# Attention and a gated feed-forward block on one core: more gate products by the seven-product form, their quarters in other buffers, and GpSimd for some of the elementwise work

## The chip, the cores and the metric

The kernel runs on one core of one Trainium2 chip. The metric is device time in microseconds (us). Five engines work side by side, each through its own queue in order: TensorE (PE in profiles, with its weight loads as PEld), VectorE (DVE), ScalarE (ACT), GpSimd (POOL) and SyncE (SP, which here issues DMAs). An instruction waits in its engine's queue until the instructions on other engines that it depends on have ended, and everything behind it in that queue waits too.

## The reference

Inputs are q, k and v of shape (8 batches, 8 heads, 576 positions, 64) and three weights. Attention is causal in a window: heads 0 to 3 see the last 32 positions, heads 4 to 7 every fourth of the last 128. Its output, as 4608 tokens of 512, goes through a gated block:

```python
scores = scale * np.matmul(q, k.transpose(0, 1, 3, 2))
...
attn = attn / (np.sum(attn, axis=-1, keepdims=True) + 1e-09)
return np.matmul(attn, v)
...
g = x @ w_gate                                  # (4608, 512) @ (512, 1536)
gelu = 0.5 * g * (1.0 + erf(g * inv_sqrt2))
val = x @ w_val
return (gelu * val @ w_out)                     # (4608, 1536) @ (1536, 512)
```

## The kernel before

The 4608 tokens are cut into nine chunks of 512 (`CH`). Attention of a batch is computed on TensorE in 64 x 64 tiles, spread over the output phase of the chunk before it is needed; the last batch's falls in chunk 6. x is kept transposed in `x_all` (shown as xT): features on partitions, tokens in columns.

A chunk has two phases. In the gate phase the 12 blocks nb of 128 hidden units are computed. A block done directly takes four matmuls of 512 columns for the gate value (word "g": then a gelu on ScalarE from the PSUM bank) and four for the other factor (word "u": then VectorE multiplies gelu and factor from the bank into `u_all`). The two banks of a block come from `gate_banks`. In the output phase `u_all` is multiplied by w_out.

From chunk 1 on, the output product is done pair by pair (two blocks are a pair j) in a form with seven block products in place of eight. It needs sums of u, made by VectorE in `u_sums` (words "k"; `ux`), and the seven products run in the order 1, 7, 6, 4, 5, 2, 3, twelve matmuls of 256 columns each.

The same form is used for some gate pairs, those in `IN_SEVEN`. Per pair `ffn1_seven` emits seven groups (words "f", in the order 1, 2, 6, 7, 5, 4, 3) of four 256-column matmuls, 28 in place of 16 of 512 columns. The groups need sums of the weights (`gate_sums`, words "h", made once in a chunk before, in columns of x_all that are no longer used) and of x (`x_sums`, word "x", once for each chunk, again in freed columns). A group's result lies in one PSUM bank and `quarter_out` takes it out: products 1, 6 and 7 are copied by ScalarE into a saved buffer (`snap`, shown as vdiag and turned); products 2, 5 and 4 are added by VectorE to one of these into a quarter (128 x 512: 256 columns of gate, 256 of the other factor); product 3 is copied by ScalarE into a quarter. One group later `quarter_gelu` puts the gelu of a quarter's first half on ScalarE, and one group after that `quarter_u` multiplies it by the other half into u_all. Within a pair the groups alternate between two banks, and a group that starts a bank anew must wait until the last result there has been read.

The order of everything is written out by hand: `gate_words` and `out_words` give a string of words for each chunk, a number standing for so many matmuls, and `run_program` emits them one by one into the engines' queues.

Of the kernel before, what the change touches and what calls it, by code (L numbers as in the profile page):

```python
# [10 lines left out]
F32 = mybir.dt.float32  # L11
# [6 lines left out]
USCALE = 8.0  # L18
# [3 lines left out]
def kernel(  # L22
# [605 lines left out]
    IN_SEVEN = {c: (1,) if c < 7 else (1, 2) for c in range(3, NCH)}  # L628
    sums_at = {1: 0, 2: 2 * CH}
# [10 lines left out]

    def gate_sums(j, part):

        for m in range(2):
# [8 lines left out]
            nc.vector.tensor_tensor(out_, first, other, op)  # L652
# [9 lines left out]
    def x_sums(c):  # L662
# [3 lines left out]
        for out_, first, other in ((t2, b12, b11), (t1, b22, t2), (t3, b22, b12), (t4, b21, t1)):  # L666
            nc.vector.tensor_tensor(out_, first, other, ALU.subtract)
# [26 lines left out]
    def quarter_out(c, j, kind, bank):  # L694

        src, kept = ps[:, bank, :], {1: 0, 6: 1, 7: 2}.get(kind)
        if kept is not None:
            nc.scalar.copy(snap[kept], src)
            return
        t = osbp.tile([P, DM], F32, tag="osb", name="quarter")  # L700
        if kind == 3:
            nc.scalar.copy(t, src)
        else:
            nc.vector.tensor_tensor(t, src, snap[{2: 0, 4: 1, 5: 2}[kind]], ALU.add)  # L704
        nb, half = 2 * j + (kind in (4, 5)), int(kind in (3, 5))
        tiles.setdefault("ready", []).append((nb, half, t))

    def quarter_gelu():

        for nb, half, t in tiles.pop("ready", []):  # L710
            g = ffn.tile([P, 2 * P], F16, tag="gq")
            nc.scalar.activation(g, t[:, 0 : 2 * P], AF.Gelu)  # L712
            tiles.setdefault("gated", []).append((nb, half, t, g))

    def quarter_u():

        for nb, half, t, g in tiles.pop("gated", []):
            dst = u_all[:, nb, 2 * P * half : 2 * P * half + 2 * P]
            by = -USCALE if nb % 2 else USCALE
            nc.vector.scalar_tensor_tensor(dst, g, by, t[:, 2 * P : 4 * P], ALU.mult, ALU.mult)  # L720
# [223 lines left out]
    def gate_banks(c, nb):  # L944
# [3 lines left out]
        if c in IN_SEVEN:  # L948
            return (1, 4) if nb in ((1, 9, 11) if c < 7 else (1, 11)) else (0, 7)
# [33 lines left out]
    def run_program(c, words, mms, banks):  # L983
# [3 lines left out]
        for word in words.split():  # L987
# [27 lines left out]
            elif kind == "f":  # L1015
                j, product, place = args
                ffn1_seven(c, j, product, (1, 4)[place], product in (1, 2, 7))
                quarter_u()
                quarter_gelu()
                quarter_out(c, j, product, (1, 4)[place])  # L1020
# [31 lines left out]
    def gate_words(c):  # L1052
# [121 lines left out]
```

## Time and profile before

| | |
|---|---|
| runs | 321.05 us median of 3 (321.03 to 321.54) |
| profiled execution | 320.39 us, span 318.7 us, TensorE clock 1.00 |
| TensorE busy | 309.1 us, 97% of the span |
| VectorE busy | 240.5 us, 75% |
| ScalarE busy | 181.2 us, 57% |
| GpSimd busy | 84.2 us, 26%; none of it after chunk 5 |

A row of the timeline gives start, duration, engine, line, operation and tiles, "x4" when rows were merged, and in brackets the idle time ahead of it with what ended it. In groups of instructions the numbers behind the first bar are busy time and the mean of one in ns.

### The profile page before, as it was taken

What the parts mean: (1) busy time and instruction counts of PE and PEld (TensorE: products, weight loads), DVE (VectorE), ACT (ScalarE), POOL (GpSimd) and SP (SyncE); (2) the same over time, 40 slices, a digit from 0 to 9 for tenths busy, and PEclk for the clock granted to TensorE, in tenths of its full rate; (3) what the DMA queues carried; (4) which work ended last, traced back from release to release, by engine and by line L of the source; (5) the groups of instructions that cost most, each with busy time, mean ns of one, the idle gap of its engine ahead of it and who ended that gap; (6) DMA issues with size and microseconds to landing.
All of it is one profiled execution on the core that took longest, in us unless ns stands there. A gap on an engine that the chain in (4) does not pass through costs nothing.

```text
span 318.7 us, 8755 instructions
## 1 busy us (share of the span) xinstructions
PE 309.1 (97%) x3585; PEld 192.6 (60%) x3585; DVE 240.5 (75%) x472; ACT 181.2 (57%) x295; POOL 84.2 (26%) x134
## 2 busy tenths in 40 slices
PE   7999999999999999999999999999999999999995
PEld 4754544446844576548654775578556856576664
DVE  6763656799757787698879886978789788946862
ACT  2673476536753477448754775567655777425740
POOL 8875603402364151160215111511000000000000
PEclk9999999999999999999999999999999999999999
DMA  8999997898699997996879638965100210030004
GB/s 188 183 203 206 205 202 149 264 187 204 159 283 154 225 210 168 241 246 159 215 165 263 157 114 194 239 146 147 35 3 1 80 56 0 2 109 25 0 0 134
DMA packets 110792, 47.17 MB, mean 148 GB/s; under 512 B 83616, under 2 KB 110240, under 8 KB 110752
## 3 DMA queue, kind: packets, MB, share of 16 engines
q1 hardware_dynamic: 97248, 38.29, 52.7%
q0 software_dynamic: 12944, 7.67, 17.0%
q10 hardware_dynamic: 560, 0.66, 0.8%
q8 instruction: 28, 0.46, 0.6%
q14 instruction: 12, 0.10, 0.1%
HBM read 37.75 MB, written 9.44 MB: 148 GB/s over the span
## 4 chain that ended last, share of the span: by engine, by line
PE 83%; DVE 9%; DMA 3%; ACT 2%; issue 2%; POOL 1%; DVEq 0%
PE ps L623 45%; PE ps L799 20%; PE ps L685 7%; PE ps L458 6%; PE ps L724 3%; DVE u_all L1007 2%; DMA xT<-in_k_dram 2%; DMA out_dram<-part 1%; DVE ux L760 1%; DVE ux L765 1%; PE ps L378 1%; DVE quarter L704 1%; DVE P L493 1%; ACT P L488 1%; DVE xT L652 1%
## 5 line engine op out<-in xcount | busy, mean ns | idle before, releaser
L1002 ACT ACTIVATE g<-ps 128x512 f16<-128x512 f32 x92 | 54.8, 597 | 73.8 <-PE ps L623 72.6
L623 PE MATMUL ps<-xT,wv 128*128 128x512 f16 x368 | 95.8, 379 | 0.7 <-DVE u_all L1007 0.7
L623 PE MATMUL ps<-xT,wg 128*128 128x512 f16 x368 | 95.0, 379 | 0.1
L1007 DVE SCALAR_TENSOR_TENSOR u_all<-g,ps 128x512 f16<-128x512 f16 x92 | 62.5, 684 | 33.4 <-PE ps L623 25.8
L623 PEld LDWEIGHTS <-wv 128*128 128x128 f16 x368 | 35.9, 98 | 38.6 <-issue 2.4
L623 PEld LDWEIGHTS <-wg 128*128 128x128 f16 x368 | 35.7, 98 | 38.5 <-issue 0.2
L799 PEld LDWEIGHTS <-u_all 128*128 128x128 f16 x390 | 36.8, 98 | 7.0 <-issue 1.0
L799 PE MATMUL ps<-wx,ux 128*128 128x256 f16 x288 | 35.8, 273 | 1.2 <-DVE ux L760 0.8
L799 PE MATMUL ps<-wo,u_all 128*128 128x256 f16 (+1 forms) x294 | 35.2, 271 | 0.0
L614 DVE TENSOR_TENSOR xT<-ps,rb 128x576 f16<-128x576 f32 x32 | 29.1, 939 | 4.4 <-PE ps L458 3.6
L488 ACT ACTIVATE P<-ps 128x832 f16<-128x832 f32 (+1 forms) x32 | 25.3, 835 | 11.8 <-PE ps L458 11.7
L799 PEld LDWEIGHTS <-ux 128*128 128x128 f16 x288 | 27.5, 98 | 5.8 <-DVE ux L760 1.4
L217 POOL CAST s<-stage 128x640 f16<-128x640 f32 x24 | 17.8, 767 | 47.3 <-DMA stage<-in_q_dram 34.3
L254 POOL CAST v<-stage 128x1152 f16<-128x1152 f32 x11 | 12.6, 1147 | 62.0 <-DMA stage<-in_v_dram 62.0
L760 DVE TENSOR_TENSOR ux<-u_all 128x512 f16<-128x512 f16 x48 | 22.1, 461 | 0.8
L585 ACT ACTIVATE lg<-ps 128x576 f32<-128x576 f32 x30 | 18.8, 656 | 6.7 <-PE ps L458 3.7
L685 PE MATMUL ps<-xT 128*128 128x256 f16 x128 | 18.8, 272 | 0.4 <-DVE quarter L704 0.4
L591 ACT ACTIVATE rb<-lg 128x576 f32<-128x576 f32 x30 | 19.0, 687 | 0.1
L712 ACT ACTIVATE g<-quarter 128x256 f16<-128x256 f32 x32 | 13.2, 414 | 9.3 <-DVE quarter L704 9.0
L229 POOL CAST s<-stage 128x512 f16<-128x512 f32 x24 | 15.9, 692 | 9.1 <-DMA stage<-in_q_dram 7.1
L685 PEld LDWEIGHTS <-xT 128*128 128x128 f16 x128 | 12.5, 97 | 7.7 <-issue 1.1
L765 DVE TENSOR_TENSOR ux<-u_all,ux 128x256 f16<-128x256 f16 (+1 forms) x44 | 15.9, 362 | 1.5
(104 smaller groups left out, 352.5 us busy)
## 6 DMA issues: line engine op xcount, KB each, us to landing
out_dram<-part SPq DMA_DIRECT2D x30, 256.0 KB, 3.4
stage<-in_v_dram SPq DMA_DIRECT2D x28, 144.0 KB, 3.6
stage<-in_q_dram SPq DMA_DIRECT2D x24, 128.0 KB, 3.5
stage<-in_k_dram SPq DMA_DIRECT2D x24, 128.0 KB, 3.0
stage<-in_q_dram SPq DMA_DIRECT2D x6, 512.0 KB, 4.8
stage<-in_k_dram SPq DMA_DIRECT2D x6, 512.0 KB, 5.2
stage<-in_v_dram SPq DMA_DIRECT2D x20, 128.0 KB, 2.9
wo<-in_moe_w_out_dram POOLq DMA_DIRECT2D x3, 512.0 KB, 16.6
```

Source lines behind the costliest of these rows:

```text
L458: nc.tensor.matmul(o[cols], lhs[rows], rhs[rows], start=st, stop=end, skip_group_check=True)
L488: nc.scalar.activation(pt[:, 0 : src.shape[1]], src, AF.Exp, bias=0.0, scale=scale)
L585: nc.scalar.activation(lg, psf[:, c0 : c0 + S], AF.Ln)
L591: nc.scalar.activation(rb, tiles.pop(("lg", n)), AF.Exp, scale=-1.0)
L614: nc.vector.tensor_tensor(dst, num, rb, ALU.mult)
L623: nc.tensor.matmul(ps[:, bank, :], w[:, kc, ns], xT[kc][:, tok], start=first, stop=end)
L685: nc.tensor.matmul(ps[:, bank, 2 * P * m : 2 * P * m + 2 * P], left[:, k], right[:, k], start=first and m == 0 and k == 0, stop=k == 1, sk ...
L760: nc.vector.tensor_tensor(ux[:, j, 0:2], k0, u_all[:, 2 * j : 2 * j + 2, hi], ALU.subtract)
L765: nc.vector.tensor_tensor(ux[:, at, 2], k0[:, :, lo], ux[:, at, 1], ALU.subtract)
L799: lambda o=o, s=s[:, P * p : P * p + P], t=t[:, c0:c1], st=st, end=end: nc.tensor.matmul(o, s, t, start=st, stop=end, skip_group_check=True)
L1002: nc.scalar.activation(g, ps[:, gate_banks(c, args[0])[0], :], AF.Gelu)
L1007: nc.vector.scalar_tensor_tensor(u_all[:, nb, :], tiles.pop(("g", nb)), -USCALE if c in SEVEN and nb % 2 else USCALE, val, ALU.mult, ALU.mult)
```

## The change

Gate pairs in the seven-product form: before, pair 1 in chunks 3 to 6, pairs 1 and 2 in chunks 7 and 8. Now pair 1 in chunks 3 to 5, pairs 1 and 2 in chunk 6, pairs 1, 2 and 3 in chunks 7 and 8. Pair 2's weight sums are made in chunk 5 (before: chunk 6), pair 3's in chunk 6. The scale of 8 or -8 that `quarter_u` applied is multiplied into the other factor's weights once for each pair (`scaled`, ScalarE), so that the product needs two inputs and no scalar. From chunk 6 the products of `quarter_u` and the x sums go to GpSimd, as do the weight sums of pairs 2 and 3. Quarters lie in the buffers tagged rb and lg, which attention uses in the output phase, and no longer in the four osb buffers, from which results are stored. Groups in banks 5 and 6 save their products in `stage`. The words are written as a table: a number of groups for each place, and what follows them.

```diff
-    IN_SEVEN = {c: (1,) if c < 7 else (1, 2) for c in range(3, NCH)}
-    sums_at = {1: 0, 2: 2 * CH}
+    ONE = ((1, (1, 4)),)
+    IN_PLACES = {c: ONE for c in range(3, 6)}
+    IN_PLACES[6] = ONE + ((2, (1, 4)),)
+    IN_PLACES[7] = IN_PLACES[8] = ONE + ((2, (5, 6)), (3, (5, 6)))
+    IN_SEVEN = {c: [j for j, _ in IN_PLACES[c]] for c in IN_PLACES}
+    sums_at = {1: 0, 2: 2 * CH, 3: 3 * CH}
+    free_pool = range(6, NCH)
...
+    def scaled(j):
+
+        for n in range(2):
+            i = next(i for i, (_, end) in enumerate(WC) if 2 * j * P < end)
+            at = (2 * j + n) * P - WC[i][0]
+            block = wv_t[i][:, :, at : at + P]
+            nc.scalar.activation(block, block, AF.Copy, bias=0.0, scale=-USCALE if n else USCALE)
+
     def gate_sums(j, part):
 
+        if part == 0:
+            scaled(j)
...
-            nc.vector.tensor_tensor(out_, first, other, op)
+            (nc.vector if j == 1 else nc.gpsimd).tensor_tensor(out_, first, other, op)
...
-            nc.vector.tensor_tensor(out_, first, other, ALU.subtract)
+            (nc.gpsimd if c in free_pool else nc.vector).tensor_tensor(out_, first, other, ALU.subtract)
...
         src, kept = ps[:, bank, :], {1: 0, 6: 1, 7: 2}.get(kind)
+        saved = snap if bank in (1, 4) else [stage[:, DM * i : DM * i + DM] for i in range(3)]
...
-        t = osbp.tile([P, DM], F32, tag="osb", name="quarter")
+        n = tiles["quarters"] = tiles.get("quarters", 0) + 1
+        t = nrm.tile([P, S], F32, tag=("rb", "lg", "rb", "lg", "rb")[n % 5], bufs=(3, 2, 3, 2, 3)[n % 5], name="quarter")[:, 0:DM]
...
-            by = -USCALE if nb % 2 else USCALE
-            nc.vector.scalar_tensor_tensor(dst, g, by, t[:, 2 * P : 4 * P], ALU.mult, ALU.mult)
+            (nc.gpsimd if c in free_pool else nc.vector).tensor_tensor(dst, g, t[:, 2 * P : 4 * P], ALU.mult)
...
-            return (1, 4) if nb in ((1, 9, 11) if c < 7 else (1, 11)) else (0, 7)
+            if nb in (1, 11) or (c < 6 and nb == 9):
+                return (1, 4)
+            return (5, 6) if c > 6 and nb % 2 and len(IN_SEVEN[c]) < 3 else (0, 7)
...
+    one = (
+        [0, 1, 1, 0, 1, 1, 0, 1, 1, 0, 1, 0, 0, 0, 0],
+        "||k0@0||k2@0||||k3@0|k3@1@2|k3@2@2|U|U k4@0|k1@0 k1@1@2|k1@2@2 k4@1 k4@2",
+    )
...
+    three = ([4, 4, 4, 3, 2, 2, 2], "k0@0||||k4@0|k1@0 k2@0|U k2@1@3")
+    three_mid, three_last = "U k2@2@3", "u11 k5@0 k3@0 k5@1@3 k5@2@3"
...
+    def seven_words(c):
+
+        pairs = IN_PLACES[c]
+        orders = [[f"f{j}@{product}@{banks[n % 2]}" for n, product in enumerate((1, 2, 6, 7, 5, 4, 3))] for j, banks in pairs]
+        pairs = [j for j, _ in pairs]
+        groups = orders[0] if len(pairs) == 1 else [w for both in zip(*orders[:2]) for w in both]
+        if pairs[1:] and orders[0][0][-1] == orders[1][0][-1]:
+            groups = orders[0] + orders[1]
+        groups += orders[2] if len(pairs) > 2 else []
...
```

A slot list such as that of `three` is read so: that many groups ahead of the first direct block's g, then that many after each of the following g and u words; the string between two bars is what follows the groups there.

ScalarE's queue in the gate phase of chunk 7, from the gelu of the block that follows block 1. "COPY vdiag", "COPY turned" and "COPY stage" are saved products 1, 6 and 7, "COPY quarter" is product 3, "g<-quarter" a quarter's gelu, "g<-ps" that of a direct block. Before:

```order
L1002 ACTIVATE g<-ps 128x512
L712 ACTIVATE g<-quarter 128x256 x2
L702 COPY quarter<-ps 128x512
L712 ACTIVATE g<-quarter 128x256
L698 COPY vdiag<-ps 128x512
L1002 ACTIVATE g<-ps 128x512
```

and now:

```order
L729 ACTIVATE g<-quarter 128x256 x3
L1020 ACTIVATE g<-ps 128x512
L729 ACTIVATE g<-quarter 128x256
L719 COPY quarter<-ps 128x512
L729 ACTIVATE g<-quarter 128x256
L719 COPY quarter<-ps 128x512
L729 ACTIVATE g<-quarter 128x256
L714 COPY stage<-ps 128x512
```

Two pairs' products come in turn, so that two copies of product 3 follow each other, each behind a gelu, and the second of them stands ahead of the copy of pair 3's product 1 (stage).

VectorE's queue at the end of the same phase. "u_all<-g,ps" is a direct block's u, "quarter<-ps" a quarter's sum, "ux<-u_all" and "u_all<-ux" are u sums. Before:

```order
L1007 SCALAR_TENSOR_TENSOR u_all<-g,ps 128x512
L760 TENSOR_TENSOR ux<-u_all 128x512
L765 TENSOR_TENSOR ux<-u_all,ux 128x256
L767 TENSOR_TENSOR u_all<-ux,u_all 128x256
L667 TENSOR_TENSOR xT<-xT 128x512 x4
```

and now:

```order
L721 TENSOR_TENSOR quarter<-ps,stage 128x512
L776 TENSOR_TENSOR ux<-u_all 128x512 x2
L1025 SCALAR_TENSOR_TENSOR u_all<-g,ps 128x512
L721 TENSOR_TENSOR quarter<-ps,stage 128x512
L781 TENSOR_TENSOR ux<-u_all,ux 128x3x256
L783 TENSOR_TENSOR u_all<-ux,u_all 128x3x256
L1025 SCALAR_TENSOR_TENSOR u_all<-g,ps 128x512
L776 TENSOR_TENSOR ux<-u_all 128x512 x2
L781 TENSOR_TENSOR ux<-u_all,ux 128x3x256
L783 TENSOR_TENSOR u_all<-ux,u_all 128x3x256
```

Quarter sums of pair 3 now stand among the last u words, the u sums of several pairs are one instruction, and the x sums are gone from here.

GpSimd's queue, whose last work before was the cast of v for the last batch, now goes on from there (chunk 6 and the first part of chunk 7):

```order
L254 CAST v_101<-stage 128x1152 x2
L682 TENSOR_TENSOR xT<-xT 128x512 x4
L736 TENSOR_TENSOR u_all<-g,quarter 128x256 x3
L667 TENSOR_TENSOR xT<-wg_90 128x256
L667 TENSOR_TENSOR xT<-wv_94 128x256
L667 TENSOR_TENSOR xT<-xT,wg_90 128x256
L667 TENSOR_TENSOR xT<-xT,wv_94 128x256
L736 TENSOR_TENSOR u_all<-g,quarter 128x256 x5
```

The x sums (L682) and the products of quarters (L736) came to it from VectorE, and the weight sums for pair 3 (L667) stand among the products of chunk 6.

62 lines of the change are left out of this document (30 added, 32 removed).

## The prediction

> **What bounds the kernel now.** I read the page first: busy shares, then the chain that ended last.
>
> ```profile
> PE 309.1 (97%) x3585; PEld 192.6 (60%) x3585; DVE 240.5 (75%) x472; ACT 181.2 (57%) x295; POOL 84.2 (26%) x134
> PE 83%; DVE 9%; DMA 3%; ACT 2%; issue 2%; POOL 1%; DVEq 0%
> ```
>
> TensorE (PE) is busy 97% of the span and holds 83% of the chain. So a column of matmul that goes is worth its time, and a wait that TensorE meets costs its whole length. Next came the chain in order of time, which prices TensorE's work (start, us, line, count; chunks 4 and 7):
>
> ```profile
> 156.40 4.32 PE ps L623 x20
> 259.31 0.87 PE ps L685 x8
> ```
>
> Twenty 512-column matmuls take 4.32 us, 0.216 each; eight of 256 columns 0.87, 0.1087 each, 0.435 for a group of four. These are the slots; the durations that single matmul rows show are longer because matmuls overlap. Then TensorE's rows in time: where a row starts later than the row before it plus its slots, TensorE waited.
>
> ```profile
> 129.56 1.03 PE L623 MATMUL ps<-xT,wv 128*128 128x512 f16 x4
> 131.00 0.60 PE L685 MATMUL ps<-xT 128*128 128x256 f16 x4 [0.41 <-DVE quarter L704]
> ...
> 136.20 1.03 PE L623 MATMUL ps<-xT,wg 128*128 128x512 f16 x4
> 137.92 1.02 PE L623 MATMUL ps<-xT,wv 128*128 128x512 f16 x4 [0.69 <-DVE u_all L1007]
> ...
> 169.66 1.03 PE L623 MATMUL ps<-xT,wg 128*128 128x512 f16 x4
> 170.72 1.02 PE L623 MATMUL ps<-xT,wv 128*128 128x512 f16 x4
> ...
> 245.65 1.03 PE L799 MATMUL ps<-wx,ux 128*128 128x256 f16 x8 [0.33 <-DVE vdiag L837]
> ...
> 254.75 1.11 PE L623 MATMUL ps<-xT,wv 128*128 128x512 f16 x4
> ...
> 276.33 1.25 PE L799 MATMUL ps<-wx,ux 128*128 128x256 f16 x10
> 278.01 1.70 PE L799 MATMUL ps<-wx,ux 128*128 128x256 f16 x14 [0.42 <-DVE ux L760]
> ...
> 284.79 1.03 PE L623 MATMUL ps<-xT,wg 128*128 128x512 f16 x4
> ...
> 305.22 1.47 PE L799 MATMUL ps<-wo,u_all 128*128 128x256 f16 x12
> ...
> 308.22 1.70 PE L799 MATMUL ps<-wx,ux 128*128 128x256 f16 x14 [0.43 <-DVE ux L760]
> ```
>
> By slots: chunk 3 loses 131.00 − (129.56 + 0.86) = 0.58 and 137.92 − (136.20 + 0.86) = 0.86, together 1.44; chunk 4 0.20 at 170.72 (chunk 5 I take at 0.15 by its likeness); chunk 6 0.5 at 245.65, where the wait is for VectorE's read of the bank. Chunk 7 runs from 254.75 to 284.79, 30.04; its work is 64 × 0.216 + 140 × 0.1087 = 29.0 (56 products of the gate, 84 of the output), so it waits 1.0, of which 278.01 − (276.33 + 10 × 0.1087) = 0.6 at the second output product. Chunk 8's gate phase takes 305.22 − 284.79 = 20.43 for 19.9 of work, and the same 0.6 follows: 1.1. In all 4.4 us stand in these chunks for the change to win, besides work.
>
> **The change, part by part.** *Work.* Three more pairs go by seven products (chunk 6 pair 2, chunks 7 and 8 pair 3): 28 × 0.1087 = 3.04 in place of 16 × 0.216 = 3.46, −0.42 each, −1.26 in all, on the path.
>
> *Banks.* Each group of products is read out of its PSUM bank by ScalarE or VectorE, and the next user of the bank waits for that. The written order now has such users directly behind each other. Chunks 3 to 5: the last product of pair 1 (product 3, bank 1) and then g9, which `gate_banks` puts into bank 1. Chunk 6: product 3 of pair 1, then product 1 of pair 2, both bank 1. Chunks 7 and 8: product 3 of pair 2, then product 1 of pair 3, both bank 5. Before, these alternate between banks. The price, from rows of chunk 7:
>
> ```profile
> 254.08 2.16 DVE L614 TENSOR_TENSOR xT<-ps,rb 128x576 f16<-128x576 f32 x2 [0.31 <-PE ps L458]
> 258.05 0.60 ACT L1002 ACTIVATE g<-ps 128x512 f16<-128x512 f32 x1 [0.59 <-PE ps L623]
> 258.28 1.03 PE L623 MATMUL ps<-xT,wg 128*128 128x512 f16 x4
> 259.34 0.60 ACT L1002 ACTIVATE g<-ps 128x512 f16<-128x512 f32 x1 [0.70 <-PE ps L623]
> 259.84 0.58 ACT L698 COPY vdiag<-ps 128x512 f32<-128x512 f32 x1
> 260.45 0.69 DVE L704 TENSOR_TENSOR quarter<-ps,vdiag 128x512 f32<-128x512 f32 x1 [1.08 <-ACT vdiag L698]
> 261.17 0.42 ACT L712 ACTIVATE g<-quarter 128x256 f16<-128x256 f32 x1 [0.76 <-DVE quarter L704]
> 261.52 0.58 ACT L698 COPY vdiag<-ps 128x512 f32<-128x512 f32 x1
> 262.00 0.59 ACT L698 COPY turned<-ps 128x512 f32<-128x512 f32 x1
> 263.31 0.69 DVE L704 TENSOR_TENSOR quarter<-ps,turned 128x512 f32<-128x512 f32 x1 [0.22 <-PE ps L685]
> 263.92 0.68 DVE L704 TENSOR_TENSOR quarter<-ps,vdiag 128x512 f32<-128x512 f32 x1
> ```
>
> TensorE's four matmuls from 258.28 end by slots at 259.14, the gelu on them starts 0.20 later. The copy takes 0.58; VectorE goes on 0.03 after it ends. Starts follow each other by 0.50 after a gelu of 512 columns, 0.48 after a copy, 0.35 after a gelu of 256, 0.61 after VectorE's 512-column sum. So a user directly behind a copy waits at least 0.20 + 0.58 + 0.05 = 0.83, if ScalarE stands free. In chunks 3 to 5 it does (g8 and one small gelu stand ahead, both due while u8 runs): +0.83 each. Chunk 6 the same: +0.83.
>
> In chunks 7 and 8 it does not. T is time from the chunk's first matmul. The first 16 matmuls end at 3.46; product 1 of pair 1 waits for g1 on bank 1, whose matmuls end at 14 × 0.216 = 3.03, so to 3.03 + 0.20 + 0.60 + 0.04 = 3.87: +0.41 (chunk 8 orders g1 earlier: 0.07). Twelve groups and three direct blocks later product 3 of pair 2 ends at 3.87 + 14 × 0.435 + 3 × 0.865 = 12.55. VectorE has u8 at 9.3 and then the four quarter sums, 0.61 apart: 9.9, 10.5, 11.15, 11.75. ScalarE is in order: gelu of the third sum 11.87, g9 12.2, gelu of the fourth 12.7, copy of pair 1's product 3 at 13.05 to 13.63, its gelu 13.67, and only then the copy that TensorE needs, 14.0 to 14.6. Product 1 of pair 3 starts at 14.64: +2.05, in place of 0.83. Product 5 of pair 3 meets the copy of product 6 late in the same way, +0.33.
>
> All that TensorE has left of the chunk stands behind each of these stops. The end of the phase then is a chain over VectorE and ScalarE, in written order: sum of pair 3's product 5 at 19.4, two u sums (0.45 each), u10, sum of product 4 at 21.5 to 22.2, its gelu, copy of product 3 at 22.6, its gelu 23.2, g11 23.55 to 24.15, u11 24.2, u sum of pair 5 at 24.9, of pair 3 at 25.35 to 25.8. TensorE ends the gate at T = 22.3 and needs that last sum after 18 output products, at 24.3: +1.54. Before, the end looks like this (VectorE), with 0.6 lost:
>
> ```profile
> 275.23 0.68 DVE L1007 SCALAR_TENSOR_TENSOR u_all<-g,ps 128x512 f16<-128x512 f16 x1
> 276.81 0.68 DVE L1007 SCALAR_TENSOR_TENSOR u_all<-g,ps 128x512 f16<-128x512 f16 x1
> 277.52 0.42 DVE L760 TENSOR_TENSOR ux<-u_all 128x512 f16<-128x512 f16 x1
> ```
>
> Chunk 7: work 48 × 0.216 + 168 × 0.1087 = 28.6, waits 0.41 + 2.05 + 0.33 + 1.54 = 4.3, 32.9 against 30.04: +2.9. Chunk 8: waits 4.0, 32.6 against 29.0 + 1.1: +2.5.
>
> *Quarters in other buffers.* The 0.58 of chunk 3 is VectorE waiting for a store that still read the `osb` buffer; the chain shows it, and the 0.86 follows from the late VectorE.
>
> ```profile
> 125.64 4.50 DMA out_dram<-part
> 130.26 0.70 DVE quarter L704
> ```
>
> The rb and lg buffers are last read in the chunk before: −1.44. Chunks 4 and 5 lose their 0.20 and 0.15 too.
>
> *GpSimd.* It takes the u products and x sums from chunk 6 and the weight sums of pairs 2 and 3. No row shows a 256- or 512-column two-input op on it; nearest are these (mean ns behind the bar):
>
> ```profile
> L338 POOL COPY two_p<-band 64x768 f16<-64x768 f16 x2 | 1.6, 823 | 0.1
> L139 POOL TENSOR_TENSOR two_d<-late_of,class_of 64x64 f16<-64x64 f16 x2 | 0.6, 286 | 0.1
> L342 POOL COPY two_p<-band 64x64 f16<-64x64 f16 x2 | 0.5, 234 | 0.0
> ```
>
> A copy costs 0.234 + 0.837 ns per column past 64; the two-input op is 0.052 dearer at 64 columns. A u product of 256: 0.39 if as a copy, 0.60 with the 0.052 growing with the columns, which I take, being the only two-input row; a 512 sum 0.61 or 1.02.  As 12 products of 0.6 fill 7 us of 22, each has its 0.5 and more of room: 0 on the path. The x sums in chunk 7 start when VectorE has written the last attention tile (254.08 + 2.16, T = 1.5), so the first two end at 3.5 and the third at 4.6; their users are due at 6.5 and 7.4: hidden. In chunk 6 the first four sums for pair 3 stand in GpSimd's queue ahead of the product that pair 1's u sums wait for, and behind those on VectorE stand u9 and bank 7: at 0.60 the product ends at T = 15.6 as VectorE comes free at 15.7; each 0.1 more per op would cost TensorE some 0.3. The two v casts behind chunk 5's sums in that queue are used a chunk later: 0.
>
> What GpSimd does cost is VectorE's time. In chunk 4, GpSimd's cast and a u sum of VectorE start together; in chunk 7 GpSimd stands idle:
>
> ```profile
> 163.72 1.44 POOL L217 CAST s<-stage 128x640 f16<-128x640 f32 x2 [5.71 <-DMA stage<-in_q_dram]
> 163.78 0.80 DVE L765 TENSOR_TENSOR ux<-u_all,ux 128x256 f16<-128x256 f16 x1
> ...
> 262.48 0.29 DVE L765 TENSOR_TENSOR ux<-u_all,ux 128x256 f16<-128x256 f16 x1
> ```
>
> 0.80 against 0.29. The Trainium skill, SBUF — State Buffer, section Who interferes with whom, says that a VectorE instruction with two SBUF inputs and a GpSimd instruction that reads SBUF exclude each other for a whole instruction; these rows agree (0.51 lost beside a cast of 0.72). Chunk 5's eight weight sums on GpSimd now run from about T = 20.4 (they follow ScalarE's scaling) beside the u sums of pairs 1, 4 and 5, and chunk 6's last four beside those of pairs 2, 3 and 5. There VectorE has no slack (245.65). Between 0 and 4 × 0.51 = 2.0 in each; I take 0.8, since some meet nothing. Chunk 6's 0.5 and its small losses stay.
>
> *Scaling on ScalarE*, two ops in each of chunks 2, 5 and 6: no row has it. From 0.42 (the SBUF gelu of 256 columns, 261.17) to 0.60 (512 columns from PSUM); 0.6, being 512 wide. Between two gelus of direct blocks ScalarE stands idle (0.70 ahead of 259.34), and nothing but the weight sums waits: 0, at worst 0.5 in chunk 6, inside its 0.8.
>
> Sum: chunk 3 0.83 − 1.44 = −0.6; 4 0.83 − 0.20 = +0.6; 5 0.83 − 0.15 + 0.8 = +1.5; 6 −0.42 + 0.83 + 0.8 = +1.2; 7 +2.9; 8 +2.5. Together +8.1 on the profiled execution's 320.39 us (span 318.7 and 1.7 around it) is 328.5; the median of the runs, 321.05, stands 0.66 higher: 329.0.
>
> **The rivals.** *Faster: waits only trade places.* If each bank wait is 0.83 at most and the extra stop gives VectorE and ScalarE the time that they lack, all 4.4 us of old waits go, at −1.26 + 6 × 0.83 − 4.4 = −0.7: 320.3. It decides at the copy of pair 2's product 3: it must be done by T = 13.4 rather than 14.6. For it speaks that old waits are late VectorE; against it the in-order list above, two 0.5 ops, two copies and four small gelus between 11.4 and 14.6.
>
> *GpSimd becomes the bound.* Above 1.67 us per x sum the third ends past T = 6.5 in chunk 6, its due time. At 2.2 per sum and 1.3 per product chunk 6 loses some 4.5 more and chunk 7 some 2: 335.5. For it: nothing shows the op at size. Against: that is twice the row's scaling.
>
> *VectorE and GpSimd block each other along the chain.* Six u sums stand in the end chain of chunks 7 and 8 and three GpSimd products fall there; if one meeting in each chunk costs the chain 0.51, and chunks 5 and 6 lose the full 2.0 in place of 0.8: 329.0 + 1.0 + 2.4 = 332.4. For it: the rows of 163.78. Against: the products start when a gelu ends, mostly while VectorE reads PSUM. The Trainium skill's section named above, carried through, is this case.
>
> **How the numbers follow.** Chances: forecast 0.65 (own range 326.0 to 331.5: without the 0.8s 327.4, with 0.7 less in each of chunks 7 and 8 326), waits trading 0.07, GpSimd as bound 0.09, mutual blocking 0.13, between 322 and 326 0.06. The range 325.0 to 333.0 leaves out the first two rivals and part of the last case. A measurement here tells about 0.2%, 0.64 us, from no change. Only trading waits gives faster, 0.05 of its 0.07; 0.03 same; 0.92 slower.
>
> **What would show it.** TensorE's rows: 0.8 us before g9 in chunks 3 to 5, about 2 us before product 1 of pair 3 in chunks 7 and 8, released by a ScalarE copy; about 1.5 us in the second output product; no store ahead of a quarter in chunk 3. GpSimd's u product near 0.6. I am wrong if ScalarE's copies come on time, or if GpSimd's op is several times dearer.

## The result: 4% slower, and the profile after

The changed kernel takes 334.4 us (median of 4 runs, 332.96 to 336.12) against 321.3 us (321.03 to 321.82) for the kernel before on the same chip: a ratio of 1.041, 95% interval 1.036 to 1.046. Forecast were 329.0 us and a range up to 333. The direction was right; the loss was 13 us in place of 8. In the experiments two single executions ran at a much lower mean clock (453.75 us at 0.66 in experiment 8, 357.97 us at 0.85 in experiment 10); the medians and ratios below leave them out.

The page of the changed kernel, its busy line and the engines' shares of the chain that ended last:

```profile
PE 310.4 (93%) x3621; PEld 196.7 (59%) x3621; DVE 231.4 (70%) x403; ACT 191.2 (58%) x319; POOL 132.9 (40%) x194
PE 72%; DVE 15%; ACT 7%; issue 2%; DMA 2%; POOL 1%; DVEq 0%; ACTq 0%
```

TensorE's share of the chain fell from 83% to 72%; VectorE's rose from 9 to 15 and ScalarE's from 2 to 7. GpSimd has 49 us more work and holds 1% of the chain: it is not what TensorE waits for directly. VectorE is 9 us less busy than before and yet more often waited for.

Where the time went is read from TensorE's rows, chunk by chunk (the first row of a chunk is that of its first gate matmul). Before, chunks 5 and 6; chunks 7 and 8 began at 254.75 and 284.79, in rows that the prediction shows:

```profile
189.43 1.03 PE L623 MATMUL ps<-xT,wv 128*128 128x512 f16 x4
222.07 1.03 PE L623 MATMUL ps<-xT,wv 128*128 128x512 f16 x4
```

Now, chunks 5, 6, 7 and 8:

```profile
190.11 1.03 PE L623 MATMUL ps<-xT,wv 128*128 128x512 f16 x4
225.14 1.03 PE L623 MATMUL ps<-xT,wv 128*128 128x512 f16 x4
260.07 1.11 PE L623 MATMUL ps<-xT,wv 128*128 128x512 f16 x4
296.12 1.03 PE L623 MATMUL ps<-xT,wg 128*128 128x512 f16 x4
```

Chunk 5, for one, took 222.07 − 189.43 = 32.64 and now takes 225.14 − 190.11 = 35.03. Against the forecast, in us of difference to the kernel before:

| chunk | forecast | measured | TensorE's waits now |
|---|---|---|---|
| up to 2 | 0 | +0.3 | |
| 3 | −0.6 | +0.3 | 0.83, 0.33, 0.70 |
| 4 | +0.6 | +0.1 | 0.84 |
| 5 | +1.5 | +2.4 | 0.83, 0.71, 1.05 |
| 6 | +1.2 | +2.2 | 0.83, 0.26, 0.19, 1.32, 0.70 |
| 7 | +2.9 | +6.0 | 0.41, 2.08, 0.42, 2.67, then 1.7 by a slower clock |
| 8 | +2.5 | +2.4 | 2.09, 0.42, 1.25 |
| sum | +8.1 | +13.7 | 19.8 with some small ones, against 4.2 before |

The waits are again a row's start minus the row before it plus its slots. These are the rows that they are read from, as far as the text goes on to use them (chunks 3, 5 and 7):

```profile
137.26 0.60 PE L700 MATMUL ps<-xT 128*128 128x256 f16 x4
138.53 1.02 PE L623 MATMUL ps<-xT,wg 128*128 128x512 f16 x4 [0.67 <-ACT quarter L719]
...
214.38 0.39 PE L815 MATMUL ps<-wx,ux 128*128 128x256 f16 x2 [0.55 <-DVE ux L776]
215.65 1.03 PE L815 MATMUL ps<-wx,ux 128*128 128x256 f16 x8 [0.88 <-DVE vdiag L853]
...
274.80 0.38 PE L700 MATMUL ps<-xT,wg 128*128 128x256 f16 x2 [1.91 <-ACT quarter L719]
...
283.92 0.82 PE L815 MATMUL ps<-wx,ux 128*128 128x256 f16 x6
287.24 3.64 PE L815 MATMUL ps<-wx,ux 128*128 128x256 f16 x18 [2.50 <-DVE ux L776]
290.67 1.68 PE L815 MATMUL ps<-wx,u_all 128*128 128x256 f16 x12
```

At 138.53: 138.53 − (137.26 + 4 × 0.1087) = 0.83, the bank wait of chunks 3 to 6. At 287.24: 287.24 − (283.92 + 6 × 0.1087) = 2.67. From 287.24 to 290.67 stand 18 matmuls, 1.96 us by slots, and they took 3.43: TensorE ran, but slowly. A view in stretches of a microsecond shows why; its last columns are the granted TensorE clock, the DMA share and GB/s, the first figure after the length is TensorE's busy time, the third VectorE's, the fifth GpSimd's:

```profile
285.00:286.00 1.00, 0.00 (x0) 0.00 (x0) 1.00 (x2) 0.00 (x0) 0.92 (x2) 1.00 0.00 0
286.00:287.00 1.00, 0.00 (x0) 0.00 (x0) 1.00 (x1) 0.00 (x0) 1.00 (x2) 1.00 0.00 0
287.00:288.00 1.00, 0.77 (x6) 0.66 (x7) 0.97 (x2) 0.00 (x0) 1.00 (x1) 0.83 0.00 0
288.00:289.00 1.00, 1.00 (x7) 0.69 (x6) 0.97 (x2) 0.60 (x1) 1.00 (x2) 0.50 0.00 0
```

Just after the stop the clock falls to half, for 3.41 us. And while TensorE stood, VectorE and GpSimd were both busy nearly all the time. VectorE's rows there, and at the same place of chunk 8, where GpSimd has nothing more to do, and then GpSimd's row there:

```profile
284.99 2.19 DVE L776 TENSOR_TENSOR ux<-u_all 128x512 f16<-128x512 f16 x2
287.21 1.39 DVE L781 TENSOR_TENSOR ux<-u_all,ux 128x768 f16<-128x768 f16 x1
288.64 1.39 DVE L783 TENSOR_TENSOR u_all<-ux,u_all 128x768 f16<-128x768 f16 x1
...
320.68 0.76 DVE L776 TENSOR_TENSOR ux<-u_all 128x512 f16<-128x512 f16 x2
321.47 0.56 DVE L781 TENSOR_TENSOR ux<-u_all,ux 128x768 f16<-128x768 f16 x1
322.07 0.56 DVE L783 TENSOR_TENSOR u_all<-ux,u_all 128x768 f16<-128x768 f16 x1
```

```profile
284.46 5.16 POOL L682 TENSOR_TENSOR xT<-xT 128x512 f16<-128x512 f16 x4
```

GpSimd's row is the four x sums of chunk 8. Beside them four sums of VectorE take 2.19 + 1.39 + 1.39 = 4.97 us; in chunk 8 the same four take 0.76 + 0.56 + 0.56 = 1.88. The second of them is the one that TensorE waits for: 2.19 − 0.76 = 1.43 us later, and 2.67 − 1.25 = 1.42 is the difference between the two chunks' waits.

### The profile page after: what moved, and what is told of

Read it like the earlier page. It is cut to its first block, busy times and chain, and to the rows that moved or that the text cites. A ratio compares the mean times of both kernels' runs of the same rounds, so it can differ in the third digit from the quotient of the medians.

```text
span 332.4 us, 8894 instructions
## 1 busy us (share of the span) xinstructions
PE 310.4 (93%) x3621; PEld 196.7 (59%) x3621; DVE 231.4 (70%) x403; ACT 191.2 (58%) x319; POOL 132.9 (40%) x194
## 4 chain that ended last, share of the span: by engine, by line
PE 72%; DVE 15%; ACT 7%; issue 2%; DMA 2%; POOL 1%; DVEq 0%; ACTq 0%
PE ps L623 36%; PE ps L815 19%; PE ps L700 7%; PE ps L458 6%; DVE u_all L1025 4%; PE ps L740 3%; DVE ux L776 3%; DVE quarter L721 2%; ACT g L729 2%; DVE ux L781 2%; DMA xT<-in_k_dram 2%; ACT quarter L719 2%; ACT g L1020 1%; DVE vdiag L853 1%; DVE P L493 1%
## 5 line engine op out<-in xcount | busy, mean ns | idle before, releaser
L1025 DVE SCALAR_TENSOR_TENSOR u_all<-g,ps 128x512 f16<-128x512 f16 x86 | 58.7, 685 | 52.9 <-PE ps L623 39.9
L623 PE MATMUL ps<-xT,wg 128*128 128x512 f16 x344 | 88.9, 380 | 2.1 <-ACT quarter L719 2.0
L623 PE MATMUL ps<-xT,wv 128*128 128x512 f16 x344 | 89.7, 380 | 0.0
L1020 ACT ACTIVATE g<-ps 128x512 f16<-128x512 f32 x86 | 51.2, 596 | 62.0 <-PE ps L623 60.5
L736 POOL TENSOR_TENSOR u_all<-g,quarter 128x256 f16<-128x256 f16 x32 | 22.4, 707 | 39.1 <-ACT g L729 36.3
L488 ACT ACTIVATE P<-ps 128x832 f16<-128x832 f32 (+1 forms) x32 | 25.3, 834 | 13.7 <-PE ps L458 13.6
L729 ACT ACTIVATE g<-quarter 128x256 f16<-128x256 f32 x44 | 18.2, 413 | 16.9 <-DVE quarter L721 15.9
L776 DVE TENSOR_TENSOR ux<-u_all 128x512 f16<-128x512 f16 x48 | 25.0, 532 | 0.8
L700 PE MATMUL ps<-xT 128*128 128x256 f16 x176 | 24.6, 273 | 0.6 <-ACT stage L714 0.5
L700 PEld LDWEIGHTS <-xT 128*128 128x128 f16 x176 | 17.2, 98 | 8.5 <-issue 1.1
L682 POOL TENSOR_TENSOR xT<-xT 128x512 f16<-128x512 f16 x12 | 14.1, 1199 | 16.9 <-DVE xT L614 16.8
```

What stands on the lines that cost most here:

```text
L488: nc.scalar.activation(pt[:, 0 : src.shape[1]], src, AF.Exp, bias=0.0, scale=scale)
L623: nc.tensor.matmul(ps[:, bank, :], w[:, kc, ns], xT[kc][:, tok], start=first, stop=end)
L700: nc.tensor.matmul(ps[:, bank, 2 * P * m : 2 * P * m + 2 * P], left[:, k], right[:, k], start=first and m == 0 and k == 0, stop=k == 1, sk ...
L736: (nc.gpsimd if c in free_pool else nc.vector).tensor_tensor(dst, g, t[:, 2 * P : 4 * P], ALU.mult)
L776: nc.vector.tensor_tensor(ux[:, j, 0:2], k0, u_all[:, 2 * j : 2 * j + 2, hi], ALU.subtract)
L1020: nc.scalar.activation(g, ps[:, gate_banks(c, args[0])[0], :], AF.Gelu)
```

## The experiments

All times are medians. The experiments were run in three sessions, each on one chip: 1 to 4, 5 to 8, and 9 to 12. The kernel before ran in each of them beside the experiments (321.26, 321.06 and 321.11 us), and every ratio is formed with the time from the same session. The changed kernel was not run again: "back" means against its 334.4 us, from a session where the kernel before took 321.3. Three of its four runs have a mean clock of 0.990 to 0.994, the fourth 0.999.

**1. The banks.** A user of a bank follows another bank's user:

```diff
-    IN_PLACES[6] = ONE + ((2, (1, 4)),)
-    IN_PLACES[7] = IN_PLACES[8] = ONE + ((2, (5, 6)), (3, (5, 6)))
+    IN_PLACES[6] = ONE + ((2, (4, 1)),)
+    IN_PLACES[7] = IN_PLACES[8] = ((1, (5, 6)), (2, (1, 4)), (3, (6, 5)))
...
-            if nb in (1, 11) or (c < 6 and nb == 9):
+            if nb in (1, 11):
                 return (1, 4)
+            if c < 6 and nb == 9:
+                return (4, 1)
...
-        if pairs[1:] and orders[0][0][-1] == orders[1][0][-1]:
+        if len(pairs) == 2:
```

The last two lines keep the order of the groups as it was.

> Changed kernel, with banks handed out so that no group or block starts the bank whose copy of product 3 has just been issued: block 9 of chunks 3 to 5 takes (4, 1), pair 2 of chunk 6 (4, 1), and in chunks 7 and 8 pair 1 takes (5, 6), pair 2 (1, 4), pair 3 (6, 5). Theory 1 (the waits come from bank reuse, and TensorE pays each in full): the four waits of 0.83 us in chunks 3 to 6, two of 2.08 in chunks 7 and 8 and 0.41 at chunk 7's first product go, 7.9 us together: 334.4 becomes 326.5, between 325.5 and 328. Rival (the waits trade places: VectorE and ScalarE are late anyway and the time comes back at the output products): 331 or more.

Measured: 330.49 us (329.75 to 332.17), ratio 1.028 (1.024 to 1.033): 3.9 us of the 13 back, half of what was expected: between the theory and the rival. The four waits of 0.83 and the 0.41 are gone from TensorE's rows; chunk 5's next wait grew from 0.71 to 1.48 and chunk 6 has a new 0.58. The 2.08 became 1.33, and now another copy is waited for:

```profile
272.37 0.58 ACT L719 COPY quarter<-ps 128x512 f32<-128x512 f32 x1
273.03 0.42 ACT L729 ACTIVATE g<-quarter 128x256 f16<-128x256 f32 x1
273.36 0.57 ACT L719 COPY quarter<-ps 128x512 f32<-128x512 f32 x1
274.01 0.42 ACT L729 ACTIVATE g<-quarter 128x256 f16<-128x256 f32 x1
274.34 0.57 ACT L714 COPY stage<-ps 128x512 f32<-128x512 f32 x1
```

```profile
274.95 0.60 PE L700 MATMUL ps<-xT 128*128 128x256 f16 x4 [1.16 <-ACT stage L714]
```

None of ScalarE's rows has an idle time in brackets: it works without a stop from 272.37 to 274.91. With the bank changed, TensorE gets one group further and then meets the same late engine. What bounds there is the list of work that ScalarE has in its queue; the bank was only where it showed.

**2. The x sums of chunk 8 on VectorE** (those of 6 and 7 stay on GpSimd):

```diff
-            (nc.gpsimd if c in free_pool else nc.vector).tensor_tensor(out_, first, other, ALU.subtract)
+            (nc.gpsimd if c in (6, 7) else nc.vector).tensor_tensor(out_, first, other, ALU.subtract)
```

> Changed kernel, with only the x sums of the last chunk (four, in chunk 7's output phase) back on VectorE. Theory 2 (these four GpSimd sums block VectorE's u sums, so that TensorE stands 2.7 us at the second output product, and the slots of 0.19 us instead of 0.109 behind it come from that long stand): the wait falls to chunk 8's 1.25 and the slow slots go with it, -1.4 and -1.5: 331.5, between 330.8 and 332.5. Rival (the wait is the written order of ScalarE's and VectorE's end chain, as the prediction had it, and GpSimd costs little): 334.4 less at most 0.5.

Measured: 331.55 us (331.42 to 335.53), ratio 1.034 (1.028 to 1.040), 2.9 us back. VectorE's two sums take 0.76 again and the wait falls from 2.67 to 1.24:

```profile
289.27 0.76 DVE L776 TENSOR_TENSOR ux<-u_all 128x512 f16<-128x512 f16 x2
```

Half of the 2.9 is this wait (1.4); the rest fits the half-clock stretch behind it: chunk 7 of this trace takes 32.95 in place of 36.05, 3.1 less, and the three runs near 331.5 have a mean clock of 0.998 to 1.0. The traced run is the fourth and slowest, 335.53 us. It is 2.7 us behind the changed kernel's trace when chunk 5 begins, and chunk 6 takes 1.6 longer with a half-clock stretch of its own; neither touches the reading of chunk 7. On VectorE, behind the last u sum, the x sums kept TensorE from nothing.

**3. All of GpSimd's new work on VectorE:**

```diff
-    free_pool = range(6, NCH)
+    free_pool = ()
...
-            (nc.vector if j == 1 else nc.gpsimd).tensor_tensor(out_, first, other, op)
+            nc.vector.tensor_tensor(out_, first, other, op)
```

With `free_pool` empty, the x sums and the products of quarters are VectorE's in every chunk.

> Changed kernel, with all that it gave to GpSimd back on VectorE: products of quarters and x sums from chunk 6, weight sums of pairs 2 and 3. Theory 2 (what GpSimd does costs VectorE as much as it takes off it): chunk 7 gains about 2.5 as when the last x sums alone go back, chunks 5 and 6 stay within 0.7 each: 331.5, between 330 and 333. Rival (VectorE needs the relief and becomes the bound of chunks 6 to 8): 336 or more.

Measured: 336.37 us (335.59 to 336.58), ratio 1.046 (1.043 to 1.049): slower still; the theory failed and the rival (336 or more) held. TensorE's waits are 20.6 us in sum, the stop at pair 3's first product has grown to 2.4, and the clock is 0.990 in three of four runs. GpSimd's work as a whole does no harm: without it the kernel is 2 us slower, so with three pairs VectorE needs the relief. What matters is which of it runs beside which work of VectorE.

**4. The quarters' buffers alone**, in the kernel before:

```diff
-        t = osbp.tile([P, DM], F32, tag="osb", name="quarter")
+        n = tiles["quarters"] = tiles.get("quarters", 0) + 1
+        t = nrm.tile([P, S], F32, tag=("rb", "lg", "rb", "lg", "rb")[n % 5], bufs=(3, 2, 3, 2, 3)[n % 5], name="quarter")[:, 0:DM]
```

> Kernel before, with one part of the change alone: quarters in the rb and lg buffers instead of osb. If the store that held an osb buffer is what delayed chunk 3 (0.58 and then 0.86): faster by 1.0 to 1.5, 319.8 to 320.3. Rival (the delay comes back elsewhere, or rb and lg are held by attention): within 0.3 of before.

Measured: 320.89 us (319.08 to 322.56, 10 runs), ratio 0.999 (0.996 to 1.002): the gain of 1.0 to 1.5 that the theory expected did not come, and 0.3 or less, as the rival had it, did. In its trace (a run of 322.21 us) chunk 3's waits of 0.58 and 0.86 are gone, but the output phase that follows has one that was not there:

```profile
146.28 0.82 PE L800 MATMUL ps<-wx,ux 128*128 128x256 f16 x6
147.46 1.03 PE L800 MATMUL ps<-wx,ux 128*128 128x256 f16 x8 [0.36 <-DVE vdiag L838]
```

147.46 − (146.28 + 6 × 0.1087) = 0.53: VectorE reads the bank late here, and it is likely that in the kernel before TensorE's stops ahead of it had hidden that. Chunk 3 is 0.32 us shorter in this trace, and chunk 4, with a new wait of 0.49 for a late u, is 0.78 longer (33.97 against 33.19).

**5. Without GpSimd's weight sums** (pairs 2 and 3), in the changed kernel:

```diff
-            (nc.vector if j == 1 else nc.gpsimd).tensor_tensor(out_, first, other, op)
+            if j == 1:
+                nc.vector.tensor_tensor(out_, first, other, op)
```

> The changed kernel without the sixteen GpSimd sums of weights (pairs 2 and 3); these products then read columns that hold old x. Theory: chunks 5 and 6 are 2.4 and 2.25 us longer than in the kernel before, of which 0.83 each is the bank wait and the rest VectorE's u sums slowed by the weight sums beside them; so about 1.5 us goes from each: 331.4 us (330.6 to 332.2). Rival: the new written order alone makes VectorE late at the ends of these chunks, and the weight sums cost nothing: 333.6 or more.

Measured: 331.46 us (329.6 to 331.82), ratio 1.031 (1.028 to 1.034): 2.9 us back, as expected from the slowed u sums. TensorE's two waits at the end of chunk 5 are gone (0.71 and 1.05), those of chunk 6 fall from 1.32 and 0.70 to 0.43. VectorE at the end of chunk 5, with the weight sums beside it and without:

```profile
211.47 0.75 DVE L781 TENSOR_TENSOR ux<-u_all,ux 128x256 f16<-128x256 f16 x1
212.25 0.64 DVE L783 TENSOR_TENSOR u_all<-ux,u_all 128x256 f16<-128x256 f16 x1
212.81 0.68 DVE L1025 SCALAR_TENSOR_TENSOR u_all<-g,ps 128x512 f16<-128x512 f16 x1
213.52 0.80 DVE L776 TENSOR_TENSOR ux<-u_all 128x512 f16<-128x512 f16 x1
```

```profile
211.47 0.28 DVE L782 TENSOR_TENSOR ux<-u_all,ux 128x256 f16<-128x256 f16 x1
211.79 0.29 DVE L784 TENSOR_TENSOR u_all<-ux,u_all 128x256 f16<-128x256 f16 x1
212.00 0.68 DVE L1026 SCALAR_TENSOR_TENSOR u_all<-g,ps 128x512 f16<-128x512 f16 x1
212.72 0.42 DVE L777 TENSOR_TENSOR ux<-u_all 128x512 f16<-128x512 f16 x1
```

The u from PSUM (third row) takes 0.68 in both: in these rows only the instructions with both inputs in SBUF are slowed. By the traces chunk 5 takes 33.27 in place of 35.03, and chunk 6 33.36 in place of 34.93.

**6. Banks and x sums together** (the edits of 1 and 2).

> Other banks (as in the first experiment) and the x sums of chunk 8 on VectorE, both together. If the two costs stand in different places, their gains add: 330.5 - 2.9 = 327.6 us (326.8 to 328.5). Rival: an earlier start of the stage only meets VectorE and ScalarE later, and the gains overlap: 329.5 or more.

Measured: 327.51 us (326.7 to 329.52), ratio 1.021 (1.018 to 1.025): the sum of the two gains. Taken together the accounts close: the profiled 318.7 us of before, less 1.26 of work and 4.2 of old waits, plus this kernel's waits of 12.1, makes 325.3; its span is 325.7.

**7. The kernel before's pairs in the new written order:**

```diff
-    IN_PLACES = {c: ONE for c in range(3, 6)}
-    IN_PLACES[6] = ONE + ((2, (1, 4)),)
-    IN_PLACES[7] = IN_PLACES[8] = ONE + ((2, (5, 6)), (3, (5, 6)))
+    IN_PLACES = {c: ONE for c in range(3, 7)}
+    IN_PLACES[7] = IN_PLACES[8] = ONE + ((2, (4, 1)),)
...
-    BLOCKS[7] = BLOCKS[8] = (*three, three_mid, three_last)
+    BLOCKS[7] = BLOCKS[8] = (*two, two_mid, two_last)
```

with pair 2's weight sums in chunk 6, as in the kernel before, and `gate_banks` to match. Pair 2's banks in chunks 7 and 8 are others than in the changed kernel too.

> The changed kernel with the pairs of the kernel before (pair 1 in chunks 3 to 6, 1 and 2 in 7 and 8), kept in the new written order, with the new buffers and GpSimd's work. If the additional pairs' queues are what chunks 7 and 8 pay (2.1 for the copy, 0.4, and 1.2 to 2.7 at the phase's end), they fall back to within 1 us of the kernel before: 324.5 us (323.5 to 326). Rival: the written order and GpSimd's work cost this much with two pairs as well: 328 or more.

Measured: 327.26 us (325.62 to 328.63), ratio 1.021 (1.017 to 1.024), between the two expectations; the theory had left out chunk 8's x sums, which GpSimd makes here too, and even earlier in VectorE's chain. Chunk 7 (first three rows) and chunk 8 (the last two) have the same queues but for them:

```profile
279.12 0.60 PE L814 MATMUL ps<-wx,ux 128*128 128x256 f16 x4
280.73 0.83 PE L814 MATMUL ps<-wx,ux 128*128 128x256 f16 x6 [1.01 <-DVE ux L775]
283.54 1.70 PE L814 MATMUL ps<-wx,ux 128*128 128x256 f16 x14 [1.98 <-DVE ux L775]
...
310.68 1.47 PE L814 MATMUL ps<-wo,u_all 128*128 128x256 f16 x12
311.99 1.25 PE L814 MATMUL ps<-wx,ux 128*128 128x256 f16 x10
```

Chunk 7 waits 1.17 + 2.16 = 3.3 us there, chunk 8 not at all. VectorE's sums show the meeting again: beside these x sums one of 256 columns takes 1.19 (0.28 in chunk 8), one of 512 takes 1.26 (0.42). The rest of the loss is four bank waits of 0.83, chunk 6's weight sums (0.72 and 1.05) and 0.94 at the end of chunk 3. So with two pairs the copy wait of 2.08 is gone: in the changed kernel its place is the third pair's first product. In chunk 8, where neither bank waits nor GpSimd's x sums fall, the new order is even 0.7 us shorter than the kernel before (33.18 against 33.91); in chunks 3 to 6 it brings the bank waits. A kernel with chunk 8's queues in both chunks and other banks was not tried. The trace is of the fastest run (325.62); two of the four have a mean clock of 0.994.

**8. The u products on GpSimd alone**, in the kernel before, with `scaled` called in `gate_sums` as in the change:

```diff
-            by = -USCALE if nb % 2 else USCALE
-            nc.vector.scalar_tensor_tensor(dst, g, by, t[:, 2 * P : 4 * P], ALU.mult, ALU.mult)
+            (nc.gpsimd if c > 5 else nc.vector).tensor_tensor(dst, g, t[:, 2 * P : 4 * P], ALU.mult)
```

> The kernel before with the scale in the weights and the u products of chunks 6 to 8 on GpSimd, nothing else. Theory: with two pairs VectorE's relief is small but lies on the late u sums, so that part of the 0.6 us waits in the output phases of chunks 7 and 8 goes: 320.5 us (319.8 to 321.2). Rival: GpSimd's products run beside VectorE's u sums and slow them, so the waits grow: 322 or more.

Measured: 320.39 us (nine runs, 319.65 to 322.98), ratio 0.999 (0.996 to 1.001): as expected in size, but the interval includes no change. TensorE's 0.6 in the output phases of chunks 7 and 8 falls to 0.23 and 0.38.

**9. TensorE kept busy through the stop**: ten additional matmuls into a free bank, where it stands in chunk 7.

```diff
-            return "12 q0@1 x8 12 q1@1 12 q2@1 12 q3@0 12 q4@0 12 q5@0 12 q6@1" if c < NCH - 1 else "L"
+            return "12 q0@1 x8 6 W10@0@0 6 q1@1 12 q2@1 12 q3@0 12 q4@0 12 q5@0 12 q6@1" if c < NCH - 1 else "L"
```

> The changed kernel with ten additional 512-column matmuls (2.16 us) into the free bank 0, set where TensorE stands 2.67 us in the output phase of chunk 7. Theory: the half-clock stretch of 3.41 us after that stop comes from TensorE's standing still; filled, the stop stays about as long but the clock stays at 1.0: 332.9 us (332.3 to 333.4), clock 0.998 or more in the runs. Rival: the stretch has another cause (load, time): 334.4 and a clock of 0.994 as before.

Measured: 333.49 us (332.2 to 333.71), ratio 1.038 (1.036 to 1.041), with a clock of 0.999 or more in all four runs, against 0.994, 0.994, 0.999 and 0.990 in those of the changed kernel. The stop lasts as long (the tenth filler ends at about 287.1 and 0.5 us is still to wait), but the 18 products behind it run at their slots again, 289.70 − 287.61 = 2.09 in place of 3.43:

```profile
284.93 2.32 PE L907 MATMUL ps<-ones 128*128 128x512 f16 x10
287.61 2.25 PE L815 MATMUL ps<-wx,ux 128*128 128x256 f16 x18 [0.36 <-DVE ux L776]
289.70 1.47 PE L815 MATMUL ps<-wx,u_all 128*128 128x256 f16 x12
```

So the half clock follows from TensorE's standing still. Chunk 7 takes 34.51 in place of 36.05, 1.54 less. The median fell by 0.9 only; one of the changed kernel's four runs had no stretch either, by its clock of 0.999, and it took 332.96.

**10 and 11. What of the change is worth keeping**: the quarters' buffers and the u products on GpSimd, both in the kernel before (the edits of 4 and 8); and the same with pair 2 by seven products in chunk 6:

```diff
-    IN_SEVEN = {c: (1,) if c < 7 else (1, 2) for c in range(3, NCH)}
+    IN_SEVEN = {c: (1,) if c < 6 else (1, 2) for c in range(3, NCH)}
...
-            return (1, 4) if nb in ((1, 9, 11) if c < 7 else (1, 11)) else (0, 7)
+            return (1, 4) if nb in ((1, 9, 11) if c < 6 else (1, 11)) else (0, 7)
```

> The kernel before with two parts of the change alone, both tried singly already: quarters in the rb and lg buffers, and the scale in the weights with the u products of chunks 6 to 8 on GpSimd. If their small gains (0.4 and 0.6) add: 320.2 us (319.5 to 320.8). Rival: each was chance: 321.0.

> The same, with pair 2 also by seven products in chunk 6, in the written order of the kernel before; pair 2's weight sums then fall into chunk 5, on VectorE. Work goes by 0.42; theory: in this order no bank is met late, and TensorE keeps most of it: 319.8 us (319.2 to 320.5). Rival: VectorE, with the u sums of chunk 5 and 6 already late (0.5 lost in chunk 6), pays more than 0.42: 320.8 or more.

Measured for the first: 320.00 us (eleven runs, 319.22 to 320.59), ratio 0.9973 (0.9957 to 0.9989). It is 0.3% faster than the kernel before, as expected from the two small gains. Where the gain lies the trace doesn't show: chunk 3 is 0.51 us shorter than before, chunk 4 0.46 longer, chunk 8 0.34 shorter. For the second: 321.91 us (320.89 to 322.99), ratio 1.003 (1.001 to 1.005): 1.9 us slower than the first, for 0.42 of work saved; the rival held. Chunk 5 takes 33.94 against 32.58 of the first, chunk 6 33.14 against 32.65. Pair 2's weight sums, eight in 1.6 us of VectorE, now stand in chunk 5 among the last u's, and its end is late:

```profile
207.91 0.68 DVE L1017 SCALAR_TENSOR_TENSOR u_all<-g,ps 128x512 f16<-128x512 f16 x1
208.51 0.28 DVE L662 TENSOR_TENSOR xT<-wg 128x256 f16<-128x256 f16 x1
...
209.32 0.68 DVE L1017 SCALAR_TENSOR_TENSOR u_all<-g,ps 128x512 f16<-128x512 f16 x1
```

TensorE waits 0.47 and 0.92 there.

**12. Chunk 5's weight sums earlier**, on top of experiment 6:

```diff
-    BLOCKS[5] = (one[0], one[1].replace("|k1@0", "|h2@0 h2@1 k1@0").replace("|k1@2", "|h2@2 h2@3 k1@2"), "", "")
+    BLOCKS[5] = (one[0], "||k0@0||k2@0|h2@0|h2@1|h2@2|k3@0 h2@3|k3@1@2|k3@2@2|U|U k4@0|k1@0 k1@1@2|k1@2@2 k4@1 k4@2", "", "")
```

> Other banks and x sums of chunk 8 on VectorE, and chunk 5's eight GpSimd weight sums some 7 us earlier, from behind block 6's gate value on, so that they end before VectorE's last u sums. Theory: what they cost is where they stand, and most of chunk 5's 1.5 us goes: 327.5 - 1.5 = 326.0 us (325.2 to 326.9). Rival: they slow VectorE wherever they run, and the delay is carried to the end: 327.5.

Measured: 327.51 us (326.82 to 327.93), ratio 1.020 (1.017 to 1.022), the same as experiment 6: the rival held. The sums came only 2 us earlier, not 7: GpSimd begins them at 206.25, right behind its casts and copies for attention, and runs them without a gap to 212.6 (experiment 6: to 214.5). VectorE meets them with other instructions (two u products of 0.42 now take 0.89 and 0.92, two u sums 1.69 in place of 0.75), is free of them by 212.6, and is as late in the end: chunk 5's waits are 0.38, 1.05, 0.60 and 0.70 in place of 1.48 and 1.05. Moving the words moved the meeting and not the loss. Whether sums made before 206 would be free was not tried: GpSimd's casts stand there.

## Why the prediction was right in sign and too small

*The bank waits came out as worked out.* Four of 0.83, two of 2.08 (forecast 2.05), 0.41, and 0.42 (0.33). ScalarE's queue in chunk 7 went as the sum had it, with nothing between:

```profile
273.19 0.58 ACT L719 COPY quarter<-ps 128x512 f32<-128x512 f32 x1
273.86 0.42 ACT L729 ACTIVATE g<-quarter 128x256 f16<-128x256 f32 x1
274.18 0.57 ACT L719 COPY quarter<-ps 128x512 f32<-128x512 f32 x1
```

The chunk begins at 260.07, so the second copy ends at T = 14.7 (forecast 14.6), and product 1 of pair 3 starts at 14.73 (14.64). Two slips of the sum are small: 14.64 − 12.55 is 2.09 and not 2.05, and 328.5 with the 0.66 added is 329.15 and not 329.0. The rival "waits only trade places" needed the copy by T = 13.4 and falls, and experiment 1 shows how deep the cause lies: freeing the bank regained 0.75 of the 2.08.

*"0 on the path" for the x sums failed.* The step looked at the x sums of the chunk in which they are used (three of them done by T = 4.6, hidden; all four were done by 5.0, and nothing waited). It never placed those of chunk 8. They are written behind the first twelve output products of chunk 7 and, on VectorE, stood behind the last u sum. In GpSimd's queue there is nothing to keep them back, so they start at 284.46, on top of the chain that ends the gate phase. Instead of 1.54 the wait was 2.67 (experiment 2 took it to 1.24). So the step that failed is the overlap: moved to GpSimd, these sums ran beside the u sums that TensorE waits for, at 1.43 us of waiting and, by the stop's length, some 1.7 of half clock. This is the rival "block each other along the chain" with another partner than it named: it had the u products.

*The 0.8 for the weight sums in chunks 5 and 6 was mis-sized.* Chunk 5's two waits were 1.76 and chunk 6's 2.0; without the sums they are none and 0.43. The sums cost 1.76 and about 1.6, near the bound of 2.0 that was kept for the range, not the middle. The reason given for 0.8, that some meet nothing, was wrong: seven of chunk 5's eight sums follow each other without a gap beside a busy VectorE, and experiment 12 shows that one other place is no better. The rule weighed there (the Trainium skill, SBUF — State Buffer, section Who interferes with whom: the two exclude each other for a whole instruction, and the one that issues first has it) agrees with the rows in part. VectorE is held up by up to the length of one GpSimd sum: 0.56 became 1.39, 0.83 more, beside sums of 1.29 (5.16 / 4). But four VectorE sums (1.88 alone) and four GpSimd sums (4.6 at the undisturbed 1.15) would take 6.5 us one after the other, and they took 5.6 (284.46 to 290.03), so by these rows the exclusion is not complete. Nor is the loss shared: GpSimd's four took 0.56 longer than undisturbed, and VectorE lost 3.1.

*The clock was not in the forecast at all*: it cost 1.7 us in the profiled chunk 7, and 0.9 in the median by experiment 9.

*Of chunk 3's −1.44 less than a third stayed.* The 0.58 and 0.86 did go, but 0.33 and 0.70 came behind them in the output phase; experiment 4 shows the second (0.53) with the buffers alone. "Where a stall goes, what is late next" was asked of chunk 7 and not here.

*Chunk 4 was forecast too high.* It came at +0.1 in place of +0.6: its bank wait did come (0.84), and it regained something else that no row was found for. *GpSimd's work was dearer than taken, at no cost by itself.* A u product took 0.67 undisturbed (forecast 0.60) and an x sum 1.15 (1.02); the means are 0.71 and 1.20:

```profile
L736 POOL TENSOR_TENSOR u_all<-g,quarter 128x256 f16<-128x256 f16 x32 | 22.4, 707 | 39.1 <-ACT g L729 36.3 <-PE ps L623 2.4
L682 POOL TENSOR_TENSOR xT<-xT 128x512 f16<-128x512 f16 x12 | 14.1, 1199 | 16.9 <-DVE xT L614 16.8
```

The profiled loss exceeds the forecast's 8.1 by 5.6 us: 3.1 of it in chunk 7 (x sums 1.1, clock 1.7), 1.9 in chunks 5 and 6, 1.2 in and ahead of chunk 3, less 0.5 in chunk 4 and 0.1 in chunk 8.

## What to carry to other kernels

Work given to an idle engine is priced by what it runs beside: place every piece of it in time on the new queue, above all what only another queue's order had held back, and see which of the chain's instructions it meets. A series of moved instructions that stands without gaps beside a late engine can cost that engine as much as doing the work itself would (eight weight sums: 1.6 us of VectorE when it makes them, 1.8 us of waits at the end of chunk 5 when GpSimd does). And a stop of the engine that bounds can cost more than its length: here 2.67 us of standing brought up to 1.7 us of half clock behind it.

## What the runs showed of the hardware

TensorE's clock fell to 0.50 for 3.41 us after stops well under 3 us: 2.67 us in the changed kernel, 2.68 in experiments 1 and 5, 2.4 in experiment 3; in the profiled run of experiment 2 after stops of about 1.3 and 0.7 close together. It didn't after the 2.08 of the changed kernel's chunk 7, nor after that kernel's 1.32 and 0.70 in chunk 6; and in experiment 3 the 2.43 of chunk 7 brought a stretch while an equal 2.43 in chunk 8 did not. So a length alone doesn't decide it. It matters where the stop falls. In each of these five traces the clock goes to half and back only at whole multiples of 3.413 us from the first entry of the clock record (in the changed kernel that entry is at 4.36 and the fall at 287.67, 83 times 3.413 later). Cut into windows by this grid, the one ahead of the fall held 2.50 us of standing in the changed kernel, 2.51 in experiment 1, 2.50 in experiment 5, 2.26 in experiment 3, and 1.69 in experiment 2. The 2.43 of experiment 3's chunk 8 lay across a border, with 1.87 in one window, and windows with up to 1.95 (experiment 6) brought no fall. No single value divides all of them, since 1.69 was enough once. The grid stands differently in each run (its first entry is at 4.36 to 6.06 us in these five), which would explain why the same kernel's runs have different mean clocks; that was not tested. Filled with matmuls (experiment 9), the same stop left the clock at 1.0 in every run. The Trainium skill (TensorE: Matmul & The Clock Gate, section Part 1: The HAM clock gate) speaks of a free-running window of about 3.4 us and of half rate after an idle one. The length of the stretch and the fixed grid agree; that a whole idle window is needed doesn't agree with these runs, where TensorE stood for half to three quarters of one.

An instruction of VectorE with both inputs in SBUF, next to a running GpSimd instruction with two such inputs, took 1.39 us in place of 0.56 (768 columns), about 1.1 in place of 0.38 to 0.42 (512) and 0.75 in place of 0.28 (256). What is added goes with GpSimd's instruction more than with VectorE's own size: beside x sums of 1.2 to 1.3 us it was 0.7 to 0.95 for 256 (experiment 7), 512 and 768 columns, beside weight sums of 0.66 to 0.85 it was 0.35 to 0.5 for 256 and 512.
